# Seven products of quarters for the second projection of blocks 2 to 8, one listed order for all steps, and stores of 128 rows

## The chip, the cores and the metric

The kernel runs on one core of a Trainium2 chip. The time is the device time of one execution in microseconds (us). The engines are TensorE (PE, matmuls; its weight loads are shown apart as PEld), VectorE (DVE), ScalarE (ACT), GpSimd (POOL) and SyncE (SP, which here only issues DMAs and waits for them). Every engine takes its instructions in the order in which the program gives them. PE reads its operands from SBUF and writes to PSUM, which has eight banks of 512 fp32 numbers per partition; DVE and ACT take results out of PSUM, POOL works from SBUF to SBUF.

## The reference

Eight sequences of 576 tokens, eight heads of 64, go through an attention with a decay for each head; the result, 4608 tokens of 512 features, goes through a feed-forward part:

```python
scores = scale * np.matmul(q, k.transpose(0, 1, 3, 2))
gamma = 1.0 - 2.0 ** (-5.0 - np.arange(H, dtype=np.float32))
Dmat = np.where(rel >= 0, gamma[:, None, None] ** rel[None, :, :], 0.0)
ret = scores * Dmat[None, :, :, :]
attn_out = np.matmul(ret, v)
x = attn_out.transpose(0, 2, 1, 3).reshape(B * S, H * D)
...
h = x @ w_in
s = np.sin(alpha * h)
g = h + s * s / (alpha + 1e-09)
out = g @ w_out
```

`h = x @ w_in` (512 to 2048 features) is called the first projection here, `g @ w_out` (2048 to 512) the second.

## The kernel before

The tokens are worked on in nine blocks of 512. Blocks 0 to 7 are the first 512 tokens of each sequence; block 8 holds the last 64 tokens of all eight. All matmuls take fp16 and add up in fp32 in PSUM.

*Attention of one block.* `load` (L109) brings q, k and v by SP's queue, 256 tokens at a time, two neighbouring tokens in one row of 128 partitions. `cast` (L132) turns them to fp16, with the decays multiplied into q and k. q and k are transposed, for blocks 0 and 1 by PE (`turn`, `take`), later by DMA (`crossed`, L187). `outer` (L269) makes sums of k times v over chunks of 128 tokens; `to_state`, `more`, `chain` (L315 to L326) turn these into the decayed states of the chunks before. `scores` (L332) and `masked` (L350) make the masked scores of a chunk; `values` (L362) multiplies them by v and `add_states` (L395) adds the part that comes from earlier chunks, into the same PSUM tile `o`. The matmuls of the values come in two groups, which use the rows of the other and of the same half; the second group waits for the first, by `told` (L234), an empty instruction on POOL, or by `change_rows`. In `o` the even tokens of a chunk stand ahead of the odd ones. `keep` (L413) copies `o` to `xT`, the fp16 input of the first projection. `Ends` (L426) does the same for block 8.

*Feed-forward of one block.* The 2048 inner features are 16 units of 128. For each unit `project` (L511) makes `hps`, 128 features by 512 tokens, with four matmuls of 512 columns; `sine` (L524, ACT), `square` (L532, on DVE, ACT or POOL as the caller says) and `product` (L541, DVE) turn it into `gT[n][:, u, :]`. For the second projection `gemm2` (L557) takes a unit of four inner tiles for one of the four groups of 128 tokens: four matmuls with `gT` as weights and 512 columns of `w_out16` moving; four calls fill one PSUM bank. `finish` (L551) copies the bank to `osb`, and because even and odd tokens stand apart, it stores it with two DMAs of 64 rows each.

*Order.* The program is one sequence written out by hand; each engine's queue is that sequence with the other engines' steps left out. Blocks 0 to 2 are written step by step, blocks 3 to 8 by a loop: in each round, one `project` of block n, the attention's pieces of block n+1 that are due, and one `gemm2` of block n-1. PSUM tiles go by tags: `h0` to `h2` and `op` of one bank, `m0` and `m1` of two banks each. SBUF tiles go round in pools (`raw` 6, `s` 4, `ss` 4, `osb` 4). The last block's second projection ends the program; its last tile is split in 320 and 192 columns, copied by ACT and DVE and stored from SP's and ACT's queues:

```python
for cols, eng in ((slice(0, 320), A_), (slice(320, 512), V)):
    tag = next(h)
    for u in range(12, 16):
        gemm2(NBLK - 1, u, tag, cols)
    finish(NBLK - 1, 3, eng, cols, (nc.sync, nc.scalar))
```

At the start, while the first loads come, `keep_busy` (L572) runs matmuls on zeros whose results nobody reads.

Of the kernel before, what the change touches and what calls it, by code (L numbers as in the profile page):

```python
# [10 lines left out]
F32 = mybir.dt.float32  # L11
F16 = mybir.dt.float16
ADD = mybir.AluOpType.add
MULT = mybir.AluOpType.mult


@with_exitstack
def kernel(
# [10 lines left out]

# [9 lines left out]
    NBLK = NT // 512  # L44
    HALVED = 5
# [19 lines left out]
    work = ctx.enter_context(tc.tile_pool(name="w", bufs=1))  # L65
    psum = ctx.enter_context(tc.tile_pool(name="p", bufs=1, space=bass.MemoryType.PSUM))

    ident = const.tile([P, P], F16, tag="ident", bufs=1)
    mask = const.tile([P, 8 * 64], F16, tag="mask", bufs=1)
    cn = const.tile([P, 68], F32, tag="cn", bufs=1)  # L70
# [3 lines left out]
    eye = const.tile([16, 16], F32, tag="eye", bufs=1)  # L74
    alpha_r = const.tile([FC, P], F32, tag="alpha_r", bufs=1)
    alpha_t = const.tile([P, FC], F32, tag="alpha", bufs=1)
    inva = const.tile([P, FC], F32, tag="inva", bufs=1)
    w_in16 = const.tile([P, KT, FF], F16, tag="w_in16", bufs=1)
    w_out16 = const.tile([P, FC, 512], F16, tag="w_out16", bufs=1)
    sS = const.tile([P, B, 4, D], F16, tag="sS", bufs=1)  # L80
    xS = const.tile([P, KT, 512], F16, tag="xS", bufs=1)
# [4 lines left out]

    V, A_, G_ = nc.vector, nc.scalar, nc.gpsimd

    def load_w_in(g):
        cols = slice(g * 512, (g + 1) * 512)  # L90
        nc.gpsimd.dma_start(w_in16[:, :, cols], w_in_r[:, :, cols])

    def load_w_out(g):
        nc.gpsimd.dma_start(w_out16[:, 4 * g : 4 * g + 4, :], w_out_r[:, 4 * g : 4 * g + 4, :])
# [4 lines left out]
    def copy(eng, d_, s_):  # L99
        if eng is nc.scalar:  # L100
            eng.copy(d_, s_)  # L101
        else:
            eng.tensor_copy(d_, s_)  # L103

    raw = {}
    half = {}
    T = {}

    def load(b, nm, p):  # L109
        if p < 2 and b >= HALVED and nm != "q":  # L110
            t_ = work.tile([P, H, 2 * D], F32, tag="raw", bufs=6, name=nm + "32")
            for g in range(2):
                for r in range(2):
                    s0 = 256 * p + 128 * g + 64 * r
                    nc.sync.dma_start(  # L115
                        t_[halves(g), :, r * D : r * D + D], src[nm][b, :, s0 : s0 + 64, :].rearrange("h i d -> i h d")
                    )
        elif p < 2:
            t_ = work.tile([P, H, 2 * D], F32, tag="raw", bufs=6, name=nm + "32")
            nc.sync.dma_start(  # L120
                t_, src[nm][b, :, 256 * p : 256 * p + 256, :].rearrange("h (i r) d -> i h (r d)", r=2)
            )
        else:
            if b % 2 == 0:
                raw[b, nm, 2] = work.tile([P, H, D], F32, tag="raws", bufs=3, name=nm + "s32")
            t_ = raw[b - b % 2, nm, 2]
            nc.sync.dma_start(t_[halves(b % 2)], src[nm][b, :, 512:576, :].rearrange("h i d -> i h d"))
        raw[b, nm, p] = t_

    nbuf = {"k": 4, "q": 3, "v": 4}  # L130

    def cast(b, nm, p, eng, ys=(0, 1)):  # L132
        t_ = raw[b, nm, p]
        if (b, nm, p) not in half:
            if p < 2:
                d_ = work.tile([P, 16 * D], F16, tag=nm + "16", bufs=nbuf[nm], name=nm + "16")
                d_ = (
                    d_.rearrange("p (h r d) -> p h r d", r=2, d=D)
                    if nm == "v"
                    else d_.rearrange("p (a r t d) -> p a r t d", a=4, r=2, t=2)  # L140
                )
            elif nm == "v":
                d_ = work.tile([P, H, D], F16, tag="vs16", bufs=B // 2, name="vs16")
            else:
                d_ = work.tile([P, 4, 2, D], F16, tag="qks16", bufs=2, name=nm + "s16")
            half[b, nm, p] = d_
        dst = half[b, nm, p]
        if p == 2:
            if nm == "v":
                copy(eng, dst.rearrange("p h d -> p (h d)"), t_.rearrange("p h d -> p (h d)"))  # L150
            else:
                eng.tensor_tensor(  # L152
                    dst.rearrange("p a t d -> p t a d"),
                    t_.rearrange("p (t a) d -> p t a d", t=2),
                    fac_s[nm].rearrange("p (t a) -> p t a", t=2).unsqueeze(3).to_broadcast([P, 2, 4, D]),
                    MULT,
                )
        elif nm == "v":
            h0, h1 = 4 * ys[0], 4 * ys[-1] + 4
            copy(  # L160
                eng,
                dst[:, h0:h1].rearrange("p h r d -> p (h r d)"),
                t_[:, h0:h1].rearrange("p h x -> p (h x)"),
            )
        else:
            a0, a1 = 2 * ys[0], 2 * ys[-1] + 2
            n = 2 * (a1 - a0)
            eng.tensor_tensor(  # L168
                dst[:, a0:a1].rearrange("p a r t d -> p t (a r) d"),
                t_.rearrange("p (t a) x -> p t a x", t=2)[:, :, a0:a1].rearrange("p t a (r d) -> p t (a r) d", r=2),  # L170
                fac["halved k" if nm == "k" and b >= HALVED else nm]
                .rearrange("p (t x) -> p t x", t=2)[:, :, 2 * a0 : 2 * a1]
                .unsqueeze(3)
                .to_broadcast([P, 2, n, D]),
                MULT,
            )

    def new_T(b, nm, p):
        if (b, nm, p) not in T:
            T[b, nm, p] = (  # L180
                work.tile([P, 8, P], F16, tag=nm + "T", bufs=4, name=nm + "T")
                if p < 2
                else work.tile([P, 4, P], F16, tag=nm + "Ts", bufs=B // 2, name=nm + "Ts")
            )
        return T[b, nm, p]

    def crossed(b, p, nms="kq"):  # L187
        for nm in nms:
            x = half[b, nm, p]
            x = x.rearrange("p a r t d -> p (a r t d)") if p < 2 else x.rearrange("p a t d -> p (a t d)")  # L190
            nc.sync.dma_start_transpose(new_T(b, nm, p), x)

    trs = {}

    def turn(b, nm, p, tag, ys=(0, 1)):
        if (b, nm, p) not in trs:
            trs[b, nm, p] = psum.tile([P, 1024], F16, tag=tag, bufs=1, name="tr")
        tr, x = trs[b, nm, p], half[b, nm, p]
        for a in range(2 * ys[0], 2 * ys[-1] + 2):
            for r in range(2):  # L200
                matmul(  # L201
                    tr[:, 256 * a + 128 * r : 256 * a + 128 * r + 128],
                    x[:, a, r].rearrange("p t d -> p (t d)"),
                    ident,
                    start=(a == 0 and r == 0), stop=True, is_transpose=True, skip_group_check=True,
                )

    def take(b, nm, p, eng, ys=(0, 1)):
        d_ = new_T(b, nm, p).rearrange("p x n -> p (x n)")
        cols = slice(512 * ys[0], 512 * ys[-1] + 512)  # L210
        copy(eng, d_[:, cols], trs[b, nm, p][:, cols])

    def quads(firsts, seconds):
        return [(f, s) for s in seconds for f in firsts]

    matmul = nc.tensor.matmul

    open_turns = []

    def change_rows(key):  # L220

        if key in open_turns:
            nc.tensor.drain()
            open_turns.clear()
# [9 lines left out]
    def told(last, eng):  # L234

        mark = eng.nop()
        order(mark, last)
        return mark

    class Attention:  # L240
        def __init__(self, b):
            self.b = b
            self.halved = b >= HALVED
            self.both = {}
            self.o = {}
            self.ret = {}
            self.sc = {}
            self.kv = {}
            self.tiles = {}
            self.mark = {}  # L250

        def tile(self, name, shape, dtype, bufs):
            if name not in self.tiles:
                self.tiles[name] = work.tile(shape, dtype, tag=name, bufs=bufs, name=name)
            return self.tiles[name]

        @property
        def x(self):
            xs[self.b] = self.tile("xT", [P, KT, 512], F16, 3)
            return xs[self.b]  # L260

        @property
        def kvs(self):
            return self.tile("kvs", [P, 4, 4, D], F32, 1)

        def state_of(self, c):
            return self.tile("s16", [P, 3, 4, D], F16, 2)[:, c] if c < 3 else sS[:, self.b]

# [957 lines left out]
```

## Time and profile before

| | us |
|---|---|
| median of three runs | 309.3 |
| lowest and highest | 308.53, 311.25 |
| span of the profiled execution | 309.4 |
| second projection, 512 columns (L562), PE busy, 560 matmuls | 138.9 |
| first projection, 512 columns (L519), PE busy, 480 and 64 matmuls | 120.5, 16.4 |
| sines (L527), ACT busy | 97.1 |
| products (L543), DVE busy | 106.2 |

The profile is of one execution. It gives the busy time of each engine, groups of instructions by line and form, the stages that one asks for, and the chain of work that ended last, followed back from the end. In the group rows the numbers after the count are the busy time, the mean length of one in ns, and the idle time of that engine just ahead of it with what ended it. A matmul's length runs from its start to its modelled end, and matmuls overlap: what one costs in a stream is the distance from start to start. The lines themselves stand in the prediction.

### The profile page before, as it was taken

The numbers are of one execution on the slowest core, as the hardware profiler recorded it, in microseconds if no ns is written. First come the engines' busy times: TensorE is split into PE (matmuls) and PEld (weight loads), VectorE is DVE, ScalarE is ACT, GpSimd is POOL, SyncE is SP. The second block draws the span as 40 slices with busy tenths as digits, with TensorE's granted clock in tenths as the row PEclk, the third lists the DMA queues.
The fourth block names the chain that finished last, engine by engine and source line by source line (L and its number), as shares of the span: only waits on it lengthen the run. The fifth ranks groups of instructions, "written<-read, shape, count | busy, mean of one in ns | idle before, by whom it ended". The sixth has DMA issues, their size and how long they took to land.

```text
span 309.4 us, 7922 instructions
## 1 busy us (share of the span) xinstructions
PE 296.4 (96%) x3257; PEld 150.9 (49%) x3257; DVE 207.4 (67%) x298; ACT 180.7 (58%) x286; POOL 138.4 (45%) x154
## 2 busy tenths in 40 slices
PE   6669999999999999999999999999999999999995
PEld 4546555554544544454445444544454454444443
DVE  1596799989859888666866586576656746655600
ACT  1434983766544766675677567756774456555411
POOL 5690774589449587759149722990030000000000
PEclk9776999999999999999999999999999999999999
DMA  7999999699497788987788788885431111111132
GB/s 227 335 215 217 278 260 247 160 247 303 90 289 213 88 190 183 272 140 171 161 226 209 179 163 192 230 199 132 101 72 39 34 36 36 35 34 37 42 89 73
DMA packets 115540, 49.84 MB, mean 161 GB/s; under 512 B 69792, under 2 KB 111024, under 8 KB 115504
## 3 DMA queue, kind: packets, MB, share of 16 engines
q1 hardware_dynamic: 110912, 44.97, 60.0%
q0 software_dynamic: 4224, 4.19, 8.1%
q8 instruction: 25, 0.41, 0.6%
q10 hardware_dynamic: 368, 0.18, 0.3%
q14 instruction: 11, 0.09, 0.1%
HBM read 36.74 MB, written 9.44 MB: 149 GB/s over the span
## 4 chain that ended last, share of the span: by engine, by line
PE 84%; DMA 3%; POOL 3%; SPq 3%; DVE 2%; ACT 1%; issue 1%; DVEq 0%; ACTq 0%; POOLq 0%
PE ops L562 39%; PE hps L519 37%; DMA q<-in_q_dram 3%; PE o L384 3%; PE sc L342 2%; SPq L115 2%; POOL q L168 1%; PE kv L282 1%; DVE s L316 1%; DVE ret L354 1%; PE o L406 1%; SPq L120 1%; ACT s_t L527 1%; POOL k L168 1%; PE tr L201 0%
## 5 line engine op out<-in xcount | busy, mean ns | idle before, releaser
L562 PE MATMUL ops<-w_out,gT 128*128 128x512 f16 (+2 forms) x592 | 142.4, 374 | 0.3 <-ACT kvs L101 0.2
L543 DVE SCALAR_TENSOR_TENSOR gT<-ss_t,inva,hps 128x512 f16<-128x512 f16 x144 | 106.2, 745 | 53.1 <-ACT ss_t L536 46.1
L527 ACT ACTIVATE s_t<-hps,alpha_t 128x512 f16<-128x512 f32 x144 | 97.1, 686 | 71.3 <-PE hps L519 68.8
L519 PE MATMUL hps<-xT,w_in 128*128 128x512 f16 (+1 forms) x544 | 127.7, 370 | 0.0
L519 PEld LDWEIGHTS <-w_in 128*128 128x128 f16 x608 | 59.1, 99 | 64.5 <-issue 0.9
L562 PEld LDWEIGHTS <-gT 128*128 128x128 f16 x592 | 56.2, 98 | 64.3 <-issue 0.7
L538 DVE TENSOR_TENSOR ss_t<-s_t 128x512 f16<-128x512 f16 x72 | 42.2, 587 | 19.5 <-ACT s_t L527 18.8
L536 ACT ACTIVATE ss_t<-s_t 128x512 f16<-128x512 f16 x62 | 38.8, 631 | 0.9
L354 DVE TENSOR_TENSOR ret<-sc,mask 128x1024 f16<-128x1024 f32 (+1 forms) x32 | 35.1, 1118 | 1.9 <-PE sc L342 1.8
L168 POOL TENSOR_TENSOR k<-k,cn 128x1024 f16<-128x1024 f32 (+1 forms) x13 | 22.1, 1699 | 25.0 <-DMA k<-in_k_dram 20.7
L101 ACT COPY osb<-ops 128x512 f32<-128x512 f32 (+1 forms) x34 | 19.7, 582 | 22.0 <-PE ops L562 20.6
L168 POOL TENSOR_TENSOR q<-q,cn 128x1024 f16<-128x1024 f32 (+1 forms) x16 | 27.2, 1708 | 10.1 <-DMA q<-in_q_dram 10.0
L538 POOL TENSOR_TENSOR ss_t<-s_t 128x512 f16<-128x512 f16 x10 | 10.8, 1083 | 19.5 <-ACT s_t L527 10.7
L101 ACT CAST xT<-o 128x1024 f16<-128x1024 f32 (+1 forms) x14 | 13.2, 958 | 7.9 <-PE o L406 7.8
L324 POOL TENSOR_TENSOR kvs<-s,kvs 128x256 f32<-128x256 f32 x22 | 16.1, 730 | 3.1 <-ACT kvs L101 1.4
L103 POOL CAST v<-v 128x1024 f16<-128x1024 f32 (+1 forms) x10 | 12.2, 1234 | 9.5 <-DMA v<-in_v_dram 8.4
L519 PE MATMUL hps<-xS,w_in 128*128 128x512 f16 x64 | 16.4, 379 | 0.0
L323 POOL TENSOR_TENSOR s<-kvs,cn 128x256 f32<-128x256 f32 x22 | 14.3, 651 | 0.3
L152 POOL TENSOR_TENSOR ks<-ks,cn 128x512 f16<-128x512 f32 x4 | 4.2, 1041 | 22.0 <-PE o L384 22.0
L384 PE MATMUL o<-ret,v 64*64 64x128 f16 (+1 forms) x512 | 11.9, 226 | 1.3 <-DVE ret L354 0.7
L342 PE MATMUL sc<-qT,kT 64*64 64x128 f16 (+1 forms) x512 | 10.9, 221 | 1.9 <-DVE ret L354 1.9
L316 POOL TENSOR_TENSOR s<-kvs,cn 128x256 f16<-128x256 f32 x19 | 12.2, 646 | 1.1 <-ACT kvs L101 0.5
(59 smaller groups left out, 142.3 us busy)
## 6 DMA issues: line engine op xcount, KB each, us to landing
out_dram<-osb SPq DMA_DIRECT2D x70, 128.0 KB, 2.4
q<-in_q_dram SPq DMA_DIRECT2D x16, 512.0 KB, 6.2
k<-in_k_dram SPq DMA_DIRECT2D x10, 512.0 KB, 8.2
v<-in_v_dram SPq DMA_DIRECT2D x10, 512.0 KB, 6.2
k<-in_k_dram SPq DMA_DIRECT2D x24, 128.0 KB, 3.1
v<-in_v_dram SPq DMA_DIRECT2D x24, 128.0 KB, 3.2
w_in<-in_moe_w_in_dram POOLq DMA_DIRECT2D x4, 512.0 KB, 11.3
w_out<-in_moe_w_out_dram POOLq DMA_DIRECT2D x4, 512.0 KB, 9.8
```

The lines of the kernel that those rows point to most:

```text
L101: eng.copy(d_, s_)
L168: eng.tensor_tensor(dst[:, a0:a1].rearrange("p a r t d -> p t (a r) d"), t_.rearrange("p (t a) x -> p t a x", t=2)[:, :, a0:a1].rearrange( ...
L324: nc.gpsimd.tensor_tensor(self.kvs[:, c], s32, self.kvs[:, c], ADD)
L342: matmul(sc[halves(g), t, c : c + n], kT[halves(t), 2 * a + r, halves(g)], qT[halves(t), 2 * a : 2 * a + 2, 64 * g + i0 : 64 * g + 64], st ...
L354: nc.vector.tensor_tensor(ret.rearrange("p t (z x) -> p (t z) x", z=2)[:, :, 0:n], sc.rearrange("p t (z x) -> p (t z) x", z=2)[:, :, 0:n], ...
L384: made.append(matmul(o[t][halves(e), c : c + 128].rearrange("p (r i) -> p r i", r=2)[:, :, i0:64], v16[halves(g), 4 * t + 2 * x + e, r, :] ...
L519: matmul(hps_of[n, fc][0][:, cols], w_in16[:, a, fc * P : (fc + 1) * P], xs[n][:, a, cols], start=(a == 0 and part != 1), stop=(a == KT - ...
L527: nc.scalar.activation(s_t, hps, mybir.ActivationFunctionType.Sin, bias=0.0, scale=alpha_t[:, fc : fc + 1],)
L536: nc.scalar.activation(ss_t, s_t, mybir.ActivationFunctionType.Square)
L538: eng.tensor_tensor(ss_t, s_t, s_t, MULT)
L543: nc.vector.scalar_tensor_tensor(gT[n][:, fc, :], ss_t, inva[:, fc : fc + 1], hps, MULT, ADD)
L562: matmul(ops[n, c, cols.start][:, cols], gT[n][:, fk, c * P : (c + 1) * P], w_out16[:, fk, cols], start=(fk == 0), stop=(fk == FC - 1), sk ...
```

## The change

*Seven products.* Blocks 0 and 1 keep the second projection as it was (`G2`, the same four matmuls as in `gemm2`). For blocks 2 to 8 the block's product g @ w_out is cut in quarters: tokens, inner features and output features in two halves each, so that A is 2 x 2 quarters of `gT` and B 2 x 2 quarters of `w_out16`. Sums S1 to S4 of quarters of A (`SM`) and T1 to T4 of quarters of B (`TT`, made once; T3 in place of a quarter of w_out) are made in fp16 on DVE or POOL, and seven products of 256 x 1024 by 1024 x 256 (`PP`) take the place of eight. `CP` copies four intermediate results from PSUM, `AD` adds three times a bank to such a copy, and the results are stored quarter by quarter (`OQ`):

```python
+    def SM(n, s, i, eng):
+        i *= 4
+        S = {x: of_units(big16(f"S{x}.{n}"), i, 4) for x in (2, 3) if f"S{x}.{n}" in place}
+        S[1], S[4] = quarter_a(n, 1, 0, i, 4), quarter_a(n, 0, 1, i, 4)
+        a, b, op = {
+            1: lambda: (S[1], quarter_a(n, 1, 1, i, 4), ADD),
+            2: lambda: (S[1], quarter_a(n, 0, 0, i, 4), SUB),
+            3: lambda: (quarter_a(n, 0, 0, i, 4), S[1], SUB),
+            4: lambda: (S[4], S[2], SUB),
+        }[s]()
+        return eng.tensor_tensor(S[s], a, b, op)
+    BANK_OF = {1: "X", 6: "X", 7: "X", 4: "X", 2: "Y", 5: "Z", 3: "Z"}
+    def PP(n, p, j):
+        ps = bank(f"{BANK_OF[p]}.{n}")
+        for u in (2 * j, 2 * j + 1):
...
+            for c in range(2):
+                i = matmul(
+                    ps[:, 256 * c : 256 * c + 256], left[:, 0, 128 * c : 128 * c + 128], right[:, 0, :],
+                    start=starts(f"{BANK_OF[p]}.{n}"), stop=True, skip_group_check=True,
+                )
+    KEPT = {2: ("Y", "p2"), 6: ("X", "u2"), 7: ("X", "u3"), 4: ("X", "c21")}
+    def CP(n, p, eng):
+        b, t = KEPT[p]
+        return copy(eng, mid32(f"{t}.{n}"), bank(f"{b}.{n}"))
+    SUMS = {11: ("X", "p2"), 22: ("Z", "u3"), 12: ("Z", "u2")}
+    def AD(n, c):
+        b, t = SUMS[c]
+        return nc.vector.tensor_tensor(mid32(f"{t}.{n}"), bank(f"{b}.{n}"), mid32(f"{t}.{n}"), ADD)
```

Products 1, 6, 7 and 4 add up in one bank X, 5 and 3 in Z; between them X is read.

*Token order and stores.* The values and states are written into `o` in natural token order, so that a store takes 128 whole rows (blocks 0 and 1) or a quarter block:

```python
-                                o[t][halves(e), c : c + 128].rearrange("p (r i) -> p r i", r=2)[:, :, i0:64],
+                            o[halves(e), t, c : c + 128].rearrange("p (i r) -> p r i", r=2)[:, :, i0:64],
...
-        for r in range(2):
-            issue[r].dma_start(rows_of(n, c)[r, :, cols], osb[halves(r), cols])
...
+    def OS(n, c):
+        x = rows_of(n, c)
+        return nc.sync.dma_start(x.rearrange("b s d -> (b s) d") if n == 8 else x, mid32(f"osb.{n}.{c}"))
```

The last block's quarters go by two DMAs each, all on SP.

*Order and places.* The whole program is now a text, `STEPS`, of 1468 steps, which a search with random delays has ordered. A step names what is done, on which engine (`:A`, `:V`, `:G`), and in which bank or slot its result lies: eight PSUM banks one by one, 16 large SBUF slots, 28 middle ones, 16 small ones, and two for `gT`. The second group of the values waits for an empty instruction on POOL, ACT or DVE (`RL`). Two stretches of the list, one from block 2 and the end:

```python
+SM.2.3.0:V S3.2=7; PP.2.1.0 X.2=2; SI.2.15 s.2.15=10; MA.4.2:V s32.4.2=8; PP.2.1.3; CA.5.v.1.2:V v16.5.1=15
+SQ.2.8:A ss.2.8=1; PR.3.0.2 hps.3.0=0; MB.4.2:G; SQ.2.10:A ss.2.10=15; PD.2.5; PR.3.1.2 hps.3.1=1; OS.1.1
...
+PP.8.1.1; CP.8.2:A p2.8=23; SM.8.2.0:G; PP.8.5.1; AD.8.11; PP.7.4.2; PP.8.5.2; OQ.8.11; PP.8.6.2; PP.8.6.3; PP.8.6.1
+OQ.4.22; PP.8.6.0; PP.7.4.3; CP.8.6:V u2.8=1; PP.7.3.0; SM.8.4.0:V; PP.7.3.3; PP.8.7.1; CP.7.4:V c21.7=15; PP.8.7.2
+OQ.7.21; PP.8.7.0; PP.8.7.3; OQ.5.12; PP.8.5.3; CP.8.7:A u3.8=26; OQ.6.22; PP.7.3.1; PP.8.4.3; OQ.7.22; AD.7.12
+PP.8.4.1; OQ.6.21; AD.8.22; PP.8.4.2; OQ.7.12; PP.8.4.0; SM.8.4.1:V; PP.8.3.0; OQ.8.22; CP.8.4:A c21.8=4; PP.8.3.1
+PP.8.3.3; OQ.8.21; PP.8.3.2; AD.8.12; OQ.8.12
```

(`PR` is project, `SI` sine, `SQ` square, `PD` product, `KB` keep_busy, `LD` load, `CA` cast, `SC` scores, `MK` masked, `VA` and `VB` the two groups of values, `SA` add_states, `KP` keep, `FI` and `OS` copy and store of a row group; the numbers are block, unit or chunk, and part.)

More of the change, by code (lines that the diff above doesn't have):

```diff
@@ L130 @@
[L130 to L176, printed above, removed]
@@ L193 @@
[L193 to L206, printed above, removed]
@@ L208, in take @@
[L208 to L224, printed above, removed]
+        return eng.copy(d_, s_) if eng is nc.scalar else eng.tensor_copy(d_, s_)
@@ L541, in product @@
-    def product(n, fc):
-        hps, ss_t = hps_of.pop((n, fc))
-        nc.vector.scalar_tensor_tensor(gT[n][:, fc, :], ss_t, inva[:, fc : fc + 1], hps, MULT, ADD)
-    def rows_of(n, c):
-        if n == 8:
-            return out.rearrange("(b s) d -> b s d", s=S)[2 * c : 2 * c + 2, 512:576, :]
-        r0 = 576 * n + 128 * c
-        return out[r0 : r0 + 128, :].rearrange("(i r) d -> r i d", r=2)
-    def finish(n, c, eng=None, cols=slice(0, 512), issue=(nc.sync, nc.sync)):
-        osb = work.tile([P, 512], F32, tag="osb", bufs=4, name="osb")
-        copy(eng or nc.scalar, osb[:, cols], ops[n, c, cols.start][:, cols])
-        for r in range(2):
-            issue[r].dma_start(rows_of(n, c)[r, :, cols], osb[halves(r), cols])
@@ L581, in take_alpha, with starts, CN @@
[L581 to L592 removed]
+    done = {}
+    started = set()
+    def starts(name):
+        if name in started:
+            return False
+        started.add(name)
+        return True
+    def CN():
+        return nc.scalar.dma_start(cn, cn_dram.ap())
@@ new lines, in rows_of, with G2 @@
+    def rows_of(n, c, m=1):
+        if n == 8:
+            return out.rearrange("(b s) d -> b s d", s=S)[2 * c : 2 * c + 2 * m, 512:576, :]
+        return out[576 * n + 128 * c : 576 * n + 128 * (c + m), :]
+    def G2(n, c, part):
+        for fk in range(4 * part, 4 * part + 4):
+            i = matmul(
+                bank(f"op.{n}.{c}"), g_of(n)[:, fk, c * P : (c + 1) * P], w_out16[:, fk, :],
+                start=starts(f"op.{n}.{c}"), stop=True, skip_group_check=True,
+            )
+        return i
```

1562 lines of the change are left out of this document (634 added, 928 removed).

## The prediction

> **What bounds the kernel now.** I read the page's head and slices first, then the stages, then the chain that ended last, then the groups of instructions by form.
>
> ```profile
> span 309.4 us, 7922 instructions
> PE 296.4 (96%) x3257; PEld 150.9 (49%) x3257; DVE 207.4 (67%) x298; ACT 180.7 (58%) x286; POOL 138.4 (45%) x154
> PEclk9776999999999999999999999999999999999999
> ```
>
> TensorE (PE) is busy 96% of the span; its clock is granted in full except in three slices near the start. The stages (columns: length, busy time of PE, weight loads, DVE, ACT, POOL, each with its count, then clock, DMA share, GB/s):
>
> ```profile
> 0.00:25.40 25.40, 16.74 (x328) 12.85 (x329) 14.83 (x17) 7.42 (x10) 17.51 (x29) 0.79 1.06 255
> 25.40:60.00 34.60, 34.26 (x396) 19.37 (x393) 29.86 (x52) 24.81 (x41) 19.35 (x18) 0.96 1.03 228
> 60.00:98.00 38.00, 37.90 (x501) 18.86 (x499) 31.68 (x42) 21.66 (x36) 26.11 (x29) 1.00 0.93 241
> 133.00:164.00 31.00, 31.00 (x346) 15.05 (x345) 20.77 (x28) 21.05 (x34) 17.38 (x19) 1.00 0.83 182
> 226.00:257.00 31.00, 31.00 (x408) 15.17 (x406) 19.66 (x30) 17.59 (x29) 2.77 (x3) 1.00 0.19 44
> ```
>
> From 25.4 us on PE has no gap worth naming, and DVE has slack: 20.8 of 31.0 us (67%) in a middle stage, 29.9 of 34.6 (86%) at worst. So a microsecond of matmul removed after 25.4 us is a microsecond of the span, as long as the other engines keep pace. The chain says the same:
>
> ```profile
> 3.91 6.01 DMA q<-in_q_dram
> 15.31 3.50 DVE s L316 x2
> 18.82 3.41 DVE ret L354 x3
> 25.44 3.27 PE hps L519 x12
> ...
> 112.59 0.86 PE hps L519 x4
> 113.45 0.86 PE ops L562 x4
> ...
> 291.06 14.73 PE ops L562 x84
> 305.79 0.04 DVEq L103
> ```
>
> Up to 25.44 us it is load, scaling, states and masks of block 0; then PE, in pieces of four matmuls; at 305.8 us it leaves PE for the last copy. A 512-column matmul costs 0.86/4 = 0.216 us in the stream.
>
> **The products.** Before, the second projection of one block is 64 matmuls of 512 columns: 64 x 0.216 = 13.8 us. After, seven products of 8 units by 2 row groups: 112 matmuls of 256 columns, each with its own weights. The nearest rows are the halved first projections of block 1, eight such matmuls in a row with eight weight loads:
>
> ```profile
> 54.38 1.04 PE L519 MATMUL hps<-xT,w_in 128*128 128x256 f16 x8
> 54.38:55.25 0.87, 0.87 (x8) 0.78 (x8) 1.00 0.02 5
> ```
>
> The first row starts the run; the second is the stage up to the next matmul. 0.87/8 = 0.109 us: half the columns take half the time, and the weight loads (0.78 of 0.87) still hide. So 112 x 0.109 = 12.2 us, 1.6 us less per block, **-11.3 us** over blocks 2 to 8. Blocks 0 and 1 keep 64 full matmuls. The first projection and the number of attention matmuls do not change.
>
> **The helpers.** Per block the change adds four sums of 128x1024 fp16 (in two halves each of that size, eight instructions), four copies out of PSUM and three adds from PSUM, and removes the four copies of finish(). Eight T sums are made once. The prices:
>
> ```profile
> L543 DVE SCALAR_TENSOR_TENSOR gT<-ss_t,inva,hps 128x512 f16<-128x512 f16 x144 | 106.2, 745 | 53.1 <-ACT ss_t L536 46.1 <-POOL ss_t L538 3.9
> L538 DVE TENSOR_TENSOR ss_t<-s_t 128x512 f16<-128x512 f16 x72 | 42.2, 587 | 19.5 <-ACT s_t L527 18.8
> L536 ACT ACTIVATE ss_t<-s_t 128x512 f16<-128x512 f16 x62 | 38.8, 631 | 0.9
> L101 ACT COPY osb<-ops 128x512 f32<-128x512 f32 x33 | 19.3, 587 | 20.4 <-PE ops L562 18.9 <-DMA k<-in_k_dram 0.2
> L538 POOL TENSOR_TENSOR ss_t<-s_t 128x512 f16<-128x512 f16 x10 | 10.8, 1083 | 19.5 <-ACT s_t L527 10.7 <-DVE gT L543 8.8
> L103 DVE COPY osb<-ops 128x512 f32<-128x512 f32 x2 | 1.4, 678 | 0.0
> ```
>
> A sum has no row. Its nearest is the square, also fp16 from SBUF at half the length: on DVE between one square (0.59) and two (1.17), on POOL two (2.17). I take two on both. The step list gives DVE 31 of the 56 S sums and 3 of the 8 T sums, POOL the other 30. It has 39, 76 and 29 squares on DVE, ACT and POOL, where 72, 62 and 10 were. It puts 9 of the 28 copies on DVE, 19 on ACT; all 21 adds are on DVE, priced as the product from PSUM.
>
> DVE: 207.4 - 33 x 0.587 (squares) + 34 x 1.17 (sums) + 9 x 0.68 + 21 x 0.745 = 249.5, and some 15 more because it takes 6 more bank copies at 0.68 and some 20 more of the state products at about half a copy: about 264 us. POOL: 138 + 19 x 1.08 + 30 x 2.17 = 224, less some 20 for the attention work it gives up. ACT: 181 + 14 x 0.63 - 9 x 0.59 and some 10 for casts of v, about 195. POOL and ACT stay near two thirds. DVE does not: about 249 of its 264 us fall between the start of the projections and the last product, where PE needs 309.4 - 25.4 - 3.6 - 11.3 = 269 us. That is 93%, and 86% is the most that the rows show beside a full PE. The cover of the sums is thin. What is late when it fails: product() frees a PSUM bank, so the next matmul group waits for a bank. Here I put **+3 us**, between 0 (the eight banks, now given out one by one, absorb it) and some +20 (first rival).
>
> **Handovers of a bank.** Products 1, 6, 7 and 4 share bank X. Product 6 waits until the add for the upper left quarter (0.75) has read it, 7 and 4 until a copy (0.59 or 0.68) has. Behind the waiting matmul stands the whole PE queue. The list puts other groups of four (0.44 each) between; in the thinnest place, at the end, three of them, 1.3 us against a copy and an add (0.59 + 0.75). Price 0 to 0.3 us each; it is in the 3 us. The 18 relay marks between the two row halves of the values lie on POOL (7), ACT (6) and DVE (5), where they were on POOL for the later blocks; such a mark holds its queue until PE has done the group. It was once worth 0.2 us to PE:
>
> ```profile
> PE o L384 <- POOLq L236: 0.2, 1, 0.2
> ```
>
> Cost nothing, covered by the matmuls listed between; 3 us if all 18 showed.
>
> **The start.** The state product in the chain, 3.50 us for two, moves to POOL (a POOL square of twice its elements takes 1.08), and the first masks come ahead of it. The first v load falls from third to sixth on SP's queue; the weight loads stay on POOL's, the first of them earlier. 102 idle matmuls of 256 columns (11.1 us) stand before the first projection, against 26 and 44 short ones; with the attention of block 0 the PE list ahead of it sums to about 17 us from 1.3 us on, so it cannot start before 18.3; 25.4 is the other end, if loads decide. I take 23.4, **-2 us** (-5 to 0): the state product is the row that shrinks for sure. The clock of 0.96 in the second stage is at most 0.04 x 34.6 = 1.4 us, inside these bounds. SP's loads are listed earlier (16 slots for 6), on DMA that is full until 98 us anyway; I price that at 0, -1 to +1.
>
> **The end.**
>
> ```profile
> 305.87 0.36 DVE L103 COPY osb<-ops 128x192 f32<-128x192 f32 x1 [12.01 <-PE ops L562]
> out_dram<-osb SPq DMA_DIRECT2D x70, 128.0 KB, 2.4
> out_dram<-osb SPq DMA_DIRECT2D x1, 48.0 KB, 1.8
> ```
>
> Now the span ends 309.4 - 305.8 = 3.6 us after PE: a copy of 0.36, a store of 48 KB on two queues. After: an add of 0.75, then two stores of 128 KB, both on SP: +0.4 for the add, +0.6 for the larger store (2.4 for 1.8), and the second issue in line behind the first. Eleven stores of 256 KB are listed in the last 9 us of PE; at the best slice's 335 GB/s of the page's DMA row they need 8.6 us:
>
> ```profile
> GB/s 227 335 215 217 278 260 247 160 247 303 90 289 213 88 190 183 272 140 171 161 226 209 179 163 192 230 199 132 101 72 39 34 36 36 35 34 37 42 89 73
> ```
>
> So the end costs **+2 us**, +1 if nothing queues, +4 if the stores run at 230 GB/s. One store of 128 rows for two of 64 elsewhere lightens SP and is worth nothing: stores are off the chain.
>
> **Sum.** 309.4 - 11.3 + 3 - 2 + 2 = **301.1 us**. The profiled execution (309.4) stands at the median of the runs (309.3), so no correction: **301 us**.
>
> **The rivals.**
>
> *DVE becomes the bound.* For it: 93% asked where 86% was shown, and the squares' price depends on POOL. Squares on DVE by stage, and one of them beside a POOL cast:
>
> ```profile
> 133.00:164.00 31.00, 5.74 (x7) 0.00 (x0) 1.00 0.83 182
> 226.00:257.00 31.00, 5.76 (x12) 0.00 (x0) 1.00 0.19 44
> 144.80 1.90 POOL L168 TENSOR_TENSOR k<-k,cn 128x1024 f16<-128x1024 f32 x1
> 145.30 1.68 DVE L538 TENSOR_TENSOR ss_t<-s_t 128x512 f16<-128x512 f16 x1
> ```
>
> With POOL busy 17.4 of 31 us a square takes 5.74/7 = 0.82 us, with POOL at 2.8 us 5.76/12 = 0.48; the one shown takes 1.68. After the change POOL is busy to the end, and 73 fp16 instructions on DVE are of this kind. Against it: three quarters of DVE's microseconds are other work, and my 1.17 for a sum is the upper end of its row. If DVE can hold 90%, 249/0.9 = 277 us from 23.4 on, plus 5.6 at the end: **306 us**. From there each 0.1 us more on the 73 costs 7.3/0.9 = 8 us: past 0.04 us above my price it is slower than before, past 0.08 by 1%. The Trainium skill (GPSIMD Engine Reference, Specifications) says that POOL's SBUF interfaces are shared with VectorE and contend with its instructions of two SBUF inputs. By that rule every S and T sum on DVE pays as the squares do; these rows agree with it.
>
> *The values are written at a stride (slower).* The change writes o in natural token order, every second fp32 of a PSUM bank, where runs of 64 stood.
>
> ```profile
> L384 PE MATMUL o<-ret,v 64*64 64x128 f16 x416 | 11.7, 234 | 1.3 <-DVE ret L354 0.7 <-POOLq L236 0.2
> L384 PE MATMUL o<-ret,v 64*64 64x64 f16 x96 | 3.2, 190 | 0.0
> L406 PE MATMUL o<-qT,s 64*64 64x128 f16 x192 | 5.7, 229 | 0.0
> ```
>
> No row shows a strided write. If it halves the rate, these 11.7 + 3.2 + 5.7 us, about 13 without their overlap, come again: 301 + 13 = **314 us**. It decides from a factor of 1.6 (8 us). Against it: four of these matmuls share the array, and 416 of them already take 11.7/104 = 0.11 us per four, about twice a lone 128-column pass (0.109/2), so there is room. The Trainium skill (PSUM — Partial Sum Buffer, Specifications) says that a non-contiguous pattern in PSUM slows matmuls significantly. By that rule this rival is what happens; no run here shows it.
>
> *Nothing new waits.* The banks absorb DVE, the start gains 5: 309.4 - 11.3 - 5 + 1 = **294 us**.
>
> **Chances.** Forecast (295 to 306): 0.60. DVE bound: 0.20, of which 0.07 beyond 312. Strided write: 0.09. Nothing waits: 0.11. The range goes from 294 to 312 and leaves out about 0.04 below and 0.16 above; the forecast's own range is 295 to 306. About 1% (306.2 and 312.4) is what a measurement of this kernel can tell from no change: faster 0.72 (the forecast and the last rival, and a little), within 0.12, slower 0.16.
>
> **What would show it.** Right: PE's 256-column products at 0.109 us in a full stream; first projection near 23 us; PE above 95% after it; DVE above 85% in the middle stages. DVE as bound: PE gaps released by DVE, many and short, in the stages where POOL is busiest, and fp16 sums above 1.2 us. A strided write: groups of the values and states twice as long. Wrong altogether if 256-column products with alternating banks take over 0.123 us (13.8/112), where the seven products save nothing.

## The result, and the profile after

| | before | after |
|---|---|---|
| median, us | 308.9 (307.5 to 311.3, 4 runs) | 316.6 (316.3 to 317.0, 4 runs) |
| ratio, 95% interval | | 1.0252, 1.0204 to 1.0300 |
| span of the profiled execution, us | 309.4 | 315.3 |

The change makes the kernel slower by 2.5%. The forecast was 301.1 us, with a range up to 312. Executions over 1.5% above the fastest of their kernel are left out of the medians and ratios of this document.

The page of the changed kernel, head and slices:

```profile
span 315.3 us, 8643 instructions
PE 301.4 (96%) x3609; PEld 191.0 (61%) x3609; DVE 247.3 (78%) x354; ACT 184.2 (58%) x295; POOL 200.1 (63%) x174
PEclk9999999999999999999999999999999999999999
```

PE is again busy 96% of the span, and 5.0 us longer in sum, although less is multiplied. About as much is added in the first stage (21.8 us for 16.7, idle matmuls); behind it PE is as busy as before, so something there took what the products saved. The group rows by form (count, busy time, mean ns of one) say which:

```profile
L754 PE MATMUL banks<-r,w_in 128*128 128x512 f16 x544 | 131.6, 379 | 1.7 <-DVE g L777 1.3 <-DVE h L329 0.3
L855 PE MATMUL banks<-w_out,g 128*128 128x256 f16 x336 | 44.5, 273 | 0.0
L573 PE MATMUL banks<-h 64*64 64x128 f16 x416 | 18.0, 305 | 0.3 <-DVE h L555 0.3
L606 PE MATMUL banks<-h 64*64 64x128 f16 x192 | 8.7, 305 | 1.5 <-issue 1.5
L573 PE MATMUL banks<-h 64*64 64x64 f16 x96 | 5.0, 258 | 0.0
```

L573 are the values, L606 the states added to them. They took 234, 229 and 190 ns each before; now 305, 305 and 258. The products (L855) and the first projection (L754) have the length that their width gives. The stages, at the same bounds as before (busy time of PE, weight loads, DVE, ACT, POOL with counts):

```profile
0.00:25.40 25.40, 21.84 (x351) 16.45 (x351) 13.18 (x19) 5.36 (x8) 15.92 (x29) 1.00 1.06 269
25.40:60.00 34.60, 31.50 (x384) 18.04 (x377) 28.87 (x41) 22.60 (x37) 21.50 (x19) 1.00 1.07 235
133.00:164.00 31.00, 30.00 (x395) 19.30 (x393) 24.66 (x33) 18.61 (x31) 26.90 (x21) 1.00 0.78 177
226.00:257.00 31.00, 30.71 (x356) 19.11 (x353) 29.29 (x48) 17.38 (x27) 13.53 (x11) 1.00 0.17 48
```

PE now has gaps: 3.1 us in the second stage, where it had 0.3, and 1.0 and 0.3 us in the two later ones, where it had none. And the chain at the start and the end:

```profile
13.49 2.37 DVE h L555 x2
19.89 2.40 PE banks L411 x21
28.56 3.04 PE banks L754 x20
...
292.46 18.06 PE banks L855 x164
```

The 3.50 us state product is gone from it, but 21 idle matmuls (L411) stand in it. The first real projection starts at 25.5 us, as before.

For an account that adds up, every microsecond of PE is given to the matmul that began last: the distance from one start to the next, which a wait lengthens. From the starts in the two traces:

| us | before | after | difference | forecast |
|---|---|---|---|---|
| start of the first projection | 25.4 | 25.5 | +0.2 | -2 |
| second projection | 125.4 | 117.8 | -7.6 | -11.3 |
| values and states | 10.3 | 17.6 | +7.3 | 0 |
| scores, outer products, turning, block 8's attention | 15.9 | 18.5 | +2.6 | 0 |
| first projection, idle matmuls | 128.5 | 130.8 | +2.3 | 0 |
| last matmul to the end | 3.9 | 5.0 | +1.1 | +2 |
| span | 309.4 | 315.3 | +5.9 | -8.3 |

The forecast's +3 for stalls belongs to the four middle rows together. Part of what those rows gained is stalls: counting, after each full-width matmul, what the next start is late beyond 0.216 or 0.109 us (by over 15 ns), the sum is 4.5 us before and 10.4 us after; the 4.5 contain about 1.4 us of half clock. Where the next matmul is one of 64 rows, the lateness is called a switch here: 26 switches make 2.5 us before, 45 make 5.0 us after. The rest is waits, and before also the half clock: 2.1 and 5.5 us.

An execution lasts 1.7 us longer than its span (317.0 for 315.3 here). So the profiled execution of before, with its span of 309.4 us, was the one of 311.25 us, and its clock was at half for two stretches. Its span was set beside the median of the times as if the two were the same quantity. Spans differ by 5.9 us, medians by 7.7 us; the profiled execution of before lay 2.3 us above its median, that of the changed kernel 0.4 us above its own, which explains the difference but for 0.1 us.

### The profile page after: what moved, and what is told of

Read it like the earlier page. It is cut to its first block, busy times and chain, and to the rows that moved or that the text cites. A ratio compares the mean times of both kernels' runs of the same rounds, so it can differ in the third digit from the quotient of the medians.

```text
span 315.3 us, 8643 instructions
## 1 busy us (share of the span) xinstructions
PE 301.4 (96%) x3609; PEld 191.0 (61%) x3609; DVE 247.3 (78%) x354; ACT 184.2 (58%) x295; POOL 200.1 (63%) x174
## 4 chain that ended last, share of the span: by engine, by line
PE 71%; DVE 13%; ACT 4%; DMA 3%; issue 3%; SPq 3%; POOL 2%; POOLq 0%; DVEq 0%; ACTq 0%
PE banks L754 26%; PE banks L855 20%; PE banks L790 9%; PE banks L411 4%; PE banks L573 4%; DVE g L777 4%; PE banks L542 2%; DVE h L555 2%; DVE r L838 2%; PE banks L606 2%; DVE s L773 2%; PE banks L498 2%; ACT s L772 2%; SPq L420 1%; ACT s L762 1%
## 5 line engine op out<-in xcount | busy, mean ns | idle before, releaser
L754 PE MATMUL banks<-r,w_in 128*128 128x512 f16 (+1 forms) x608 | 138.6, 368 | 1.7 <-DVE g L777 1.3
L762 ACT ACTIVATE s<-banks,alpha 128x512 f16<-128x512 f32 x144 | 94.7, 686 | 56.3 <-PE banks L754 55.0
L777 DVE SCALAR_TENSOR_TENSOR g<-s,inva,banks 128x512 f16<-128x512 f16 x144 | 102.0, 741 | 19.9 <-ACT s L772 11.2
L754 PEld LDWEIGHTS <-w_in 128*128 128x128 f16 x608 | 57.4, 98 | 54.9 <-issue 4.4
L855 PEld LDWEIGHTS <-g 128*128 128x128 f16 x560 | 53.7, 98 | 14.8 <-issue 0.6
L773 POOL TENSOR_TENSOR s<-s 128x512 f16<-128x512 f16 x29 | 32.0, 1107 | 38.4 <-ACT s L762 38.4
L447 POOL TENSOR_TENSOR h<-r,cn 128x1024 f16<-128x1024 f32 (+1 forms) x24 | 44.4, 1864 | 5.3 <-DMA r<-in_k_dram 2.8
L772 ACT ACTIVATE s<-s 128x512 f16<-128x512 f16 x76 | 46.1, 628 | 1.2
L838 POOL TENSOR_TENSOR r<-g 128x1024 f16<-128x1024 f16 x15 | 32.5, 2171 | 20.2 <-DVE g L838 10.4
L855 PE MATMUL banks<-w_out,g 128*128 128x256 f16 x336 | 44.5, 273 | 0.0
L555 DVE TENSOR_TENSOR h<-banks,mask 128x1024 f16<-128x1024 f32 (+1 forms) x32 | 35.4, 1119 | 7.2 <-PE banks L542 6.3
L855 PE MATMUL banks<-r,g 128*128 128x256 f16 x224 | 29.7, 273 | 0.0
L855 PEld LDWEIGHTS <-r 128*128 128x128 f16 x224 | 21.7, 98 | 8.1 <-POOL r L838 0.8
L790 PEld LDWEIGHTS <-g 128*128 128x128 f16 x128 | 11.7, 98 | 14.9 <-issue 2.3
L573 PE MATMUL banks<-h 64*64 64x128 f16 (+1 forms) x512 | 18.5, 296 | 0.3 <-DVE h L555 0.3
```

Of the source, the lines that this page charges most:

```text
L447: return eng.tensor_tensor(dst[:, a0:a1].rearrange("p a r t d -> p t (a r) d"), t_.rearrange("p (t a) x -> p t a x", t=2)[:, :, a0:a1].rea ...
L555: return nc.vector.tensor_tensor(ret(b, p, y).rearrange("p t (z x) -> p (t z) x", z=2)[:, :, 0:n], bank(f"sc.{b}.{p}.{y}", 2).rearrange("p ...
L573: made.append(matmul(o[halves(e), t, c : c + 128].rearrange("p (i r) -> p r i", r=2)[:, :, i0:64], v16[halves(g), 4 * t + 2 * x + e, r, :] ...
L754: i = matmul(bank(hps)[:, cols], w_in16[:, a, u * P : (u + 1) * P], x_of(n)[:, a, cols], start=starts(hps), stop=(a == KT - 1), skip_group ...
L762: return nc.scalar.activation(small(f"s.{name}")[:, cols], bank(f"hps.{name}")[:, cols], mybir.ActivationFunctionType.Sin, bias=0.0, scale ...
L772: return nc.scalar.activation(ss_t, s_t, mybir.ActivationFunctionType.Square)
```

## The experiments

The theory was that the strided write of the values and states decides the sign; the rivals were stalls behind DVE and POOL, which now have the sums to make, and the order itself. A ratio is always to the kernel before, run beside it on the same chip; the medians of the kernel before lie between 308.2 and 310.8 us there.

| | edit | median, us | ratio (interval) | span |
|---|---|---|---|---|
| e1 | no stride, stores halved | 323.3 | 1.048 (1.042 to 1.054) | 320.1 |
| e2 | kernel before with the stride | 317.9 | 1.029 (1.022 to 1.036) | 317.0 |
| e3 | no sums | 313.1 | 1.016 (1.010 to 1.023) | 311.5 |
| e4 | no stride, order made by the copy | 313.1 | 1.014 (1.007 to 1.021) | 311.2 |
| e5 | no stride, nothing else | 310.6 | 1.007 (1.003 to 1.011) | 308.1 |
| e6 | stride on the moving operand | 318.7 | 1.032 (1.025 to 1.039) | 317.2 |
| e7 | 21 idle matmuls fewer | 315.1 | 1.021 (1.014 to 1.028) | 313.7 |
| e8 | e6 and e7 | 316.4 | 1.025 (1.019 to 1.032) | 315.1 |
| e9 | e5, e3 and e7 together | 305.1 | 0.982 (0.975 to 0.988) | 301.3 |
| e10 | e4 but for block 0, and e7 | 309.9 | 0.998 (0.994 to 1.002) | 309.3 |
| e11 | e10, 14 squares moved to ACT | 312.5 | 1.005 (1.002 to 1.009) | 311.4 |
| e12 | e1 with two store queues, and e7 | 317.1 | 1.030 (1.021 to 1.039) | 320.4 |

### e2: the stride put into the kernel before

```diff
-    o[t][halves(e), c : c + 128].rearrange("p (r i) -> p r i", r=2)[:, :, i0:64],
+    o[t][halves(e), c : c + 128].rearrange("p (i r) -> p r i", r=2)[:, :, i0:64],
...
-    o[t][halves(e), c : c + 128],
+    o[t][halves(e), c : c + 128].rearrange("p (i r) -> p r i", r=2),
...
-        return out[r0 : r0 + 128, :].rearrange("(i r) d -> r i d", r=2)
+        return out[r0 : r0 + 128, :].rearrange("(r i) d -> r i d", r=2)
```

> The kernel before with one part of the change alone: the values and states are written in natural token order, at a stride of two fp32, and the two stores of 64 rows take consecutive rows. Theory 1: plus 6 to 7.5 us, ratio 1.019 to 1.025; a matmul of the values lengthens from 234 to about 305 ns as in the changed kernel. Theory 2: under 2 us, ratio below 1.006.

Its group rows, in the lines of the kernel before:

```profile
L384 PE MATMUL o<-ret,v 64*64 64x128 f16 x416 | 17.9, 324 | 1.2 <-DVE ret L354 0.7
L406 PE MATMUL o<-qT,s 64*64 64x128 f16 x192 | 8.5, 317 | 0.0
L384 PE MATMUL o<-ret,v 64*64 64x64 f16 x96 | 4.8, 258 | 0.0
```

From start to start the values and states take 17.2 us for 10.3, that is +6.9, and the kernel without any of the rest of the change becomes 2.9% slower. Their matmuls grow by 90, 88 and 68 ns where the change had 71, 76 and 68. The stores take consecutive rows with this edit; from the last matmul to the end it stays at 3.9 us. The ratio of 1.029 is above the expected 1.025, and its interval (from 1.022) overlaps the expected range. So the strided write alone costs as much as the whole change lost.

### e5 and e1: the stride taken out of the change

e5 writes each chunk into PSUM as the kernel before did, even tokens ahead of odd ones, and leaves the rest; the rows of the output stand in another order:

```diff
-    o[halves(e), t, c : c + 128].rearrange("p (i r) -> p r i", r=2)[:, :, i0:64],
+    o[halves(e), t, c : c + 128].rearrange("p (r i) -> p r i", r=2)[:, :, i0:64],
...
-    o[halves(e), t, c : c + 128].rearrange("p (i r) -> p r i", r=2),
+    o[halves(e), t, c : c + 128],
```

> The changed kernel with the values and states in runs of 64 in PSUM and nothing else touched: the stores stay single, so the even and odd tokens of each 128 stand in another order in the output. It tells the stride from the doubled stores of e1 and from the longer copies of e4. Theory 1 (the strided write costs PE 7 us): 308.5 to 311, values and states at 10 to 11 us of PE. Rival (what is freed turns into waits, as e1 and e4 could be read): 313 or more.

```profile
L573 PE MATMUL banks<-h 64*64 64x128 f16 x416 | 11.7, 221 | 0.3 <-DVE h L555 0.3
L606 PE MATMUL banks<-h 64*64 64x128 f16 x192 | 6.0, 221 | 2.7 <-issue 2.7
L573 PE MATMUL banks<-h 64*64 64x64 f16 x96 | 3.4, 189 | 0.0
```

221 ns for 305: start to start 10.6 us for 17.6, so 7.0 us of PE, and the span falls by 7.2 us. Nothing else takes its place. This is the second side of e2. But the ratio is still 1.007 (1.003 to 1.011): without the stride the change is within 1% of the kernel before, and no gain.

e1 has the same two lines and puts the rows in order with two stores of 64 rows each, both on SP:

```diff
-            return nc.sync.dma_start(x.rearrange("(c p) d -> p c d", p=P), t)
+            x = x.rearrange("(c i r) d -> r i c d", r=2, c=2)
+            nc.sync.dma_start(x[0], t[halves(0)])
+            return nc.sync.dma_start(x[1], t[halves(1)])
```

> The changed kernel with one part undone: the values and states go into o in runs of 64 as before, and each store is again two of 64 rows. Theory 1 (the strided write costs PE): in the trace of the changed kernel the values' and states' matmuls hold PE 17.6 us from start to start after the first projection, before 10.3; undone, they fall back to 10 to 11 us and the time by 6 to 8 us, to 308.5 to 311 (ratio 0.998 to 1.007). Theory 2 (VectorE and the waits of the fixed order set the time): the freed PE time turns into other gaps, the time falls by less than 2 us, to 314.5 or more. The doubled stores can cost up to 1 us at the end in either.

That expectation was missed by over 12 us. The values were as short as in e5; what came was 4.5 us at the end and stalls in the stream, which from the first projection to the last matmul takes 285.7 us where e5 has 277.4. SP's timeline at the end (start, length, line; the last matmul starts at 310.6), and PE's longest bank waits:

```profile
309.35 0.61 SPq L879 DMA_DIRECT2D out_dram<-h  x1
310.00 0.60 SPq L880 DMA_DIRECT2D out_dram<-h  x1
...
316.75 0.61 SPq L883 DMA_DIRECT2D out_dram<-h  x1
```

```profile
PE banks L754 <- DVE g L777: 4.7, 5, 3.4
PE banks L856 <- DVE g L777: 2.2, 2, 1.8
```

Each issue holds SP for 0.61 us and the next comes 0.65 us later. In the changed kernel many stores are listed close together at the end; twice as many issues there are a queue that outlives PE: 9.5 us from the last matmul to the end for 5.0.

### e12: the second half of each store on another queue

As e1, but the second store of each pair is issued by ACT's queue (`nc.scalar.dma_start(x[1], ...)`), and the idle step of e7 is left out.

> As the change, but values and states written without a stride, each store in two of 64 rows of which the second is issued by ScalarE's queue, and KB.21.256.0 left out; complete, outputs in order. Theory (the extra 12.6 us of the split stores on one queue were SyncE's 32 issues of 0.65 us in line, not the smaller transfers): with ScalarE issuing half of them the tail is back near 5 us and the waits of loads are gone: 310.7 - 1.5 = 309.2 us, up to 311 for ScalarE's issues. Rival (ScalarE waits in front of each store for VectorE's result, with sines behind it, or the smaller transfers themselves are the cost): 314 us or more.

317.1 us (two executions): the side of the rival. The trace is of an execution of 322.1 us. In it the end was cured, 6.0 us; the stream was not: 290.9 us from the first projection to the last matmul. A stretch of half clock of 3.4 us loses 1.7; two lie in this stream, one in e1's and none in e5's, which leaves 287.5, 284.0 and 277.4 us. The shortest execution of e12 has a span of 313.8 us; with the start (23.5) and the end of the trace its stream would be 284.3 us, an estimate, and so about as long as e1's and still 7 us longer than e5's. In the trace, ACT's row of waits shows copies that wait until a store has read the slot that they write, 7.7 us in all for 1.5 in e1; whether the shorter executions have these waits no trace shows:

```profile
ACT h L329 <- DMA out_dram<-h: 7.7, 3, 3.1
```

So the end of e1 was SP's line of issues. What lengthened the stream of both is not settled: it may be loads late behind the stores, or the smaller transfers.

### e4, e10 and e6: natural order made elsewhere

e4 writes PSUM without a stride, and `KP`, the copy from `o` to the fp16 input of the projection, puts the tokens in order:

```diff
-    eng, x_of(b)[:, 2 * t : 2 * t + 2, cols], bank(f"o.{b}.{p}", 2)[:, t].rearrange("p (x n) -> p x n", x=2)
+    eng,
+    x_of(b)[:, 2 * t : 2 * t + 2, cols].rearrange("p a (g i r) -> p a g r i", g=2, r=2),
+    bank(f"o.{b}.{p}", 2)[:, t].rearrange("p (x g r i) -> p x g r i", x=2, g=2, r=2),
```

> The changed kernel with the values and states in runs of 64 in PSUM, and the natural token order made by the copy to x instead (fp16 writes at a stride on ScalarE and VectorE); stores as in the change. Theory 1: as e1, 308 to 310.5, up to 1 us below e1 since no store is doubled; the copies stay at about 1.0 us for 128x1024, or up to double if the stride costs there, which the banks absorb. Theory 2: 314.5 or more.

The values and states are again short (10.7 us from start to start), but the copies are longer. The row of after, then that of e4:

```profile
L329 ACT CAST r<-banks 128x1024 f16<-128x1024 f32 x12 | 12.1, 1013 | 7.7 <-PE banks L606 5.2 <-PE banks L573 2.4
```

```profile
L329 ACT CAST r<-banks 128x1024 f16<-128x1024 f32 x12 | 15.6, 1312 | 5.0 <-PE banks L606 3.5 <-PE banks L573 1.4
```

0.3 us more on each copy of two banks, and the stalls after full-width matmuls rise from 10.4 to 13.7 us: 3.5 of the 6.0 us that e5 gains are kept. The median of 313.1 us lies between the two theories.

e10 uses this for blocks 1 to 7 and leaves the strided write in block 0, whose copies the first projection waits for; the idle step of e7 is left out too.

> Complete computation with the outputs in order: blocks 1 to 7 write values and states without a stride and let the copy KP put the tokens in order, block 0 keeps the strided write, and KB.21.256.0 is left out. Theory: the copy into natural order took 3.5 of the 5.9 us of the unstrided write for all blocks (313.1 us), part of it as stalls near the start in block 0; with block 0 as in the change and 1.5 us from the idle matmuls the time is 310.5 us, 309.5 to 312. Rival (the stalls come from the slower copies of the later blocks): 311.5 to 313.

309.9 us, 0.998 of the kernel before (0.994 to 1.002): the best complete version of the change here, with the outputs in order, and no better than before.

e6 keeps natural order and contiguous runs in PSUM, and reads the moving operand (masked scores, queries) at a stride instead:

```diff
-    ret(b, p, x)[halves(g), t, m : m + n],
+    ret(b, p, x)[halves(g), t, m : m + n].rearrange("p (r i) -> p i r", r=2),
```

> The changed kernel with the natural token order made on the reading side: the moving operand (masked scores, q) is read in the order of the tokens, at a stride of 64 or 128 fp16, and the matmuls write runs of 128 in PSUM. Theory 1 (it is the write that costs): as e5, 308.5 to 311. Rival (PE slows for any stride, reading too): values and states stay at 17 us or more, 315 to 318.

```profile
L573 PE MATMUL banks<-h 64*64 64x128 f16 x416 | 18.9, 285 | 0.3 <-DVE h L555 0.3
L606 PE MATMUL banks<-h 64*64 64x128 f16 x192 | 8.9, 285 | 1.4 <-issue 1.4
```

285 ns for e5's 221. From start to start the group takes 19.6 us, more than the 17.6 us with the strided write: reading fp16 at a stride on PE's moving side is no cheaper than writing fp32 at one. The time is on the side of the rival, 0.7 us above its range.

### e3, e7, e8 and e9: the sums and the idle matmuls

e3 leaves out the sums S and T; the products then multiply unsummed quarters, so its output is not the reference's:

```diff
+            if kind in ("SM", "TT"):
+                continue
```

> The changed kernel without the sums S and T: the seven products take unsummed quarters, so that part of the second projection is left out; VectorE loses some 27 us of work and GpSimd some 65. Theory 1: only the stalls of PE that the sums cause go, about 10.4 us of excess gaps beside 4.5 before: the time falls by 2 to 5 us, to 311.5 to 314.5. Theory 2: it falls by more than 8 us, to 308 or less.

313.1 us: 3.5 us less, all of it stalls (6.8 us of them for 10.4). DVE gives up 34 sums and POOL 30, and PE's gaps in the stage from 133 to 164 us close:

```profile
133.00:164.00 31.00, 31.00 (x403) 19.90 (x402) 22.00 (x32) 18.96 (x31) 15.23 (x16) 1.00 0.96 201
```

e7 leaves out `KB.21.256.0`, the step of 21 idle matmuls seen in the chain; e8 does this to e6.

> The changed kernel without the 21 idle matmuls (2.4 us) that stand on PE ahead of the second half of block 0's sums. Theory (these idle matmuls hold up the start, the chain runs through them): first projection at 23 to 23.5 us for 25.5, time 314 to 315. Rival (the loads of the weights, or ScalarE and VectorE in block 0, set the pace after the start): the first projection is earlier, the time within 0.7 us of the changed kernel's 316.6.

> e6 and e7 together. If both add up: 306 to 309; if the early start is eaten up: as e6.

The first projection starts at 23.9 us for 25.5 in e7 and at 24.2 for 26.1 in e8, and the medians fall by 1.5 and 2.3 us. The idle matmuls had been on the path. The 306 to 309 us expected of e8 had counted on an e6 as fast as e5.

e9 takes e5, e3 and e7 together.

> Three edits in one: values and states written without a stride (output rows in another order), the sums S and T left out (the products multiply unsummed quarters, so the output is not the reference's), and the last idle matmul step KB.21.256.0 left out. Theory (each is a cost of its own on PE): 316.6 - 5.9 - 3.5 - 1.5 = 305.7 us, 304.5 to 307, below the kernel before. Rival (the sums' stalls and the stride's time cover one another, or the fixed order gives one gain back to another wait): 308 to 311, no better than the unstrided writes alone by more than 2 us.

305.1 us. In medians the three save 6.0 + 3.5 + 1.5 = 11.0 us one by one and 316.6 - 305.1 = 11.5 together: they are costs of their own, none covers another. This kernel is 1.9% below the one before (interval of the ratio 0.975 to 0.988). Its second projection takes 115.9 us from start to start where the kernel before takes 125.4, so the seven products do pay on PE where nothing is paid for them; the first projection also starts 3.2 us earlier.

### e11: DVE relieved

e10 with 14 of the 39 squares on DVE, all in blocks 2 to 7, moved to ACT (`SQ.2.4:V` becomes `SQ.2.4:A`, and so on).

> As the kernel before it in this list (block 0 strided, the rest ordered by the copy, no KB.21.256.0), and 14 of the 39 squares on VectorE, all in blocks 2 to 7, are done on ScalarE. Theory of VectorE as the thing that the banks wait for: VectorE loses 14 x 0.585 = 8 us, the bank waits on it shrink, 309.5 us or 1 us below the kernel beside it. Rival (the stalls come from the fixed order of the list, or ScalarE becomes late in its place): no change or slower, 310.5 to 312.

312.5 us beside 309.9 for e10: no gain, but 2.6 us more. DVE is busy for 239.6 us instead of 246.0 and the stalls go from 14.1 to 16.1 us. The rows of waits show DVE's products waiting longer for squares that ACT now makes. First e10, then e11:

```profile
DVE g L793 <- POOL s L789: 11.8, 11, 2.0
```

```profile
DVE g L793 <- ACT s L788: 16.0, 20, 2.4
DVE g L793 <- POOL s L789: 12.5, 10, 2.3
```

So less work on DVE did not make PE wait less. That it is not DVE's sum of work that makes PE wait, but when a square or a sum is ready in a fixed order, fits these rows; it is argued from them and not shown by a run of its own.

## Why the prediction was wrong

*The product price was right.* The products stand 0.109 us apart, and 112 x 7 of them have a floor of 85.6 us. They took 89.3: 3.7 us of stalls and of switches to attention matmuls, which account for the way from -11.3 to -7.6.

*The failed step is the rival "The values are written at a stride (slower)", given 0.09.* The sum put this write at nothing. Its mechanism was named and is what happened; its chance was far too small, and its size (+13) too large. Measured from start to start it costs 7.3 us here, 6.9 in e2, 7.0 in e5: a factor of 1.7 (the mean lengths, which overlap, grow by 1.3), above the 1.6 from which it was to decide, though a little less than the 8 us that stood beside that factor. The forecast took a doubling of 13 us; what grew by 1.7 was 10.3 us, the time from start to start. The argument against it was that four of these matmuls share the array and so "there is room". That was inferred from lengths, 11.7/104 = 0.11 us per four, and no row showed that a slower write would fit into them. From start to start four of them take 0.072 us before and 0.116 us after (352 behind the start, 6.29 and 10.18 us): the lengths had overlapped already, and the slower write did not fit. The Trainium skill (PSUM — Partial Sum Buffer, Specifications) says that a non-contiguous pattern slows matmuls significantly; the prediction quoted the rule and gave it less weight than an argument without a row. The three runs agree with the rule and give the size: 305 to 324 ns for 221 to 234.

*What the stride leaves open.* With 7.3 us added the forecast's sum is 308.4 us, no change. The span measured is 14.2 us above the forecast; the other 6.9 us are the products (3.7), the start (2.2), and the attention and the first projection (2.6 and 2.3) against the 3 us that stood for stalls, less 0.9 at the end. The paragraphs below take these in turn.

*"DVE becomes the bound" did not happen.* DVE was priced at 264 us and was busy for 247. An S sum took 0.7 to 1.1 us on DVE, below the 1.17 taken:

```profile
L838 DVE TENSOR_TENSOR r<-g 128x1024 f16<-128x1024 f16 x13 | 13.8, 1065 | 0.0
L838 DVE TENSOR_TENSOR g<-g 128x1024 f16<-128x1024 f16 x10 | 7.0, 716 | 0.3
L838 POOL TENSOR_TENSOR r<-g 128x1024 f16<-128x1024 f16 x15 | 32.5, 2171 | 20.2 <-DVE g L838 10.4
```

The stages do not speak for a bound either: from 133 to 164 us PE loses 1.0 us with DVE at 24.7 of 31 (80%), and from 226 to 257 us it loses 0.3 with DVE at 29.3 (94%). A share of busy time above 90% was survivable; a late result in a fixed order was not. The squares on DVE take 585 ns here and 501 ns in e3, where POOL and DVE make no sums. The rule of the Trainium skill (GPSIMD Engine Reference, Specifications) on shared SBUF interfaces agrees with that in direction; 39 squares by 0.084 us are 3.3 us of DVE, which was not the bound.

*The stalls, +3.* They grew by 5.9 us, or by about 7.3 with before's half clock set aside. Switches are 2.5 of it, and without the sums 3.6 are gone (e3). The largest is one that the prediction did not look for: the old second projection of block 0 waits for a product of DVE, and does so with and without the sums:

```profile
44.16 1.02 PE L790 MATMUL banks<-w_out,g 128*128 128x512 f16 x4 [1.33 <-DVE g L777]
```

*The attention's cost, taken as unchanged.* Scores and outer products cost 2.1 us more for the same matmuls. Two waits among them, 0.96 and 0.71 us from start to start, are 0.9 us more than the two longest before; for the rest, the list goes from scores back to full-width matmuls 20 times for 14. Turning costs 0.5 us more, because 32 of its 64 matmuls stand behind the start for 24. The way into the small matmuls comes on top: after a full-width matmul the first of them starts 93 ns later (median) than a full-width one would, 45 times for 26. The table gives that time to the full-width rows. An order with fewer switches was not tried.

*The start, -2.* The state product did leave the chain, as argued. But the idle matmuls, which the prediction had in its earliest start of 18.3 us, stand in the chain: it put them at 11.1 us, and from start to start they took 14.4. With 21 of them gone (e7) the first projection starts at 23.9 us, close to the 23.4 forecast.

*The end, +2*: +1.1. That one store of 128 rows for two of 64 is worth nothing does not hold for this list: taking it back (e1) costs 4.5 us at the end alone.

## What to carry to other kernels

Before a layout change moves a stride to an operand of TensorE, price it as lost PE time on every matmul that reads or writes it; here a factor of 1.7 on a group worth 3% of the span cost 7.3 us where the products saved 7.6. When a rule speaks against a step and only an argument without a measured row speaks for it, give the rule the larger chance. Saved multiplications become saved time only where the sums that they need are ready when the list says; and SP's issues are a queue with a length, which counts at the end of a program.

## What the runs showed that was not expected

A 64x128 fp16 matmul that writes every second fp32 of a PSUM bank lasts 305 to 324 ns for 221 to 234; reading its moving fp16 operand at a stride, 285 ns. An ACT copy of two banks that writes fp16 at a stride takes 1.31 us for 1.01. A store of half the bytes holds SP no shorter: 0.61 us for each of the 128 KB in e1, 0.51 (median of 24) for the quarters of 256 KB in the changed kernel. In most of the profiles the granted clock fell to half in one to three stretches of 3.4 or 6.8 us before the last matmul, in those of the changed kernel, e3 and e5 not at all; what decides that was not tried.
